# Reordered first loads, paired K and V loads, a hinted end branch and a rearranged last block in a grouped-query attention kernel

## The chip, the cores and the metric

The kernel runs on one core of a Trainium2 chip. The metric is device time in microseconds (us) of one execution; the median over several executions is compared. Besides that there is one profiled execution, whose trace gives the rows used here.

## What is computed

Two independent problems, A and B, have the same shapes. Each takes x (16 batches, 80 rows, 576 columns), a K and a V cache (16 batches, 16 heads, 512 positions, 128 deep), and the matrices Wq (576 x 4096) and Wo (4096 x 576), all in bf16. There are 32 query heads, two to each K/V head.

```python
q = (x @ wq).reshape(B, Sq, Hq, Dh).transpose(0, 2, 1, 3)
k = jnp.repeat(k_cache, rep, axis=1)
v = jnp.repeat(v_cache, rep, axis=1)
scores = jnp.einsum("bhqd,bhkd->bhqk", q, k) * (Dh ** -0.5)
p = softmax(scores, axis=-1)
o = jnp.einsum("bhqk,bhkd->bhqd", p, v)
result = o.transpose(0, 2, 1, 3).reshape(B, Sq, Hq * Dh) @ wo
```

The two results stand side by side in the output (16, 80, 1152).

## The kernel before

The work is cut into 128 **units** U: one batch and four K/V heads. U runs over the two problems, then four groups of heads (`q`), then 16 batches. Each unit loads one K block (`ldk`, a DMA transpose of 512 KB into one of five slots of `kT`) and one V block (`ldv`, a plain DMA of 512 KB into one of three slots of `v_in`), which POOL copies into one of five slots of `v_sb` (`vp`). Four units make a window W (32 of them), and eight units make an output block h8 (16 of them).

On TensorE (PE) these jobs alternate:

- `qp m.i`: one of 8 Q projections of block m (four batches), five matmuls over 576 rows of x and Wq, evacuated into `qT`. Chunks 0 to 3 of x come from one DMA transpose (`ldx`), the fifth from another (`ldx..b`).
- `s n`: three score matmuls, followed by an exponential on ScalarE (ACT) into `P`.
- `pv U.g`: four matmuls of P and V over the first 128 query columns; `pr W`: the remaining 32 columns of four units in 64 small matmuls. VectorE (DVE) then takes the reciprocal of the row sums and scales (`rcp`, `nrm`).
- `tr W.u`: four PE transposes, copied by DVE into `oM` or, for u = 4, into `oR`.
- `op h8.n`: eight matmuls with Wo. n counts five tiles `ti` with two halves `ch` each. Tile 4 reads `oR`, the others `oM`. DVE or ACT adds the result into `acc`; in the last head group the sum goes to `osb`, from which stores (`st`) write the output.

All the order is fixed when the program is built. Every operation has a **key**, a virtual time in which a unit takes 16; the operations of each engine are issued in the order of keys, and a class `_Sched` derives the semaphore waits from what is read and written. An engine never passes a waiting instruction of its own. The constants that set keys are lists at the top: `X_T` for x blocks, `K_T` and `V_T` for the first K and V loads, `WO_T` and `W1_T` for Wo of the first head group and Wq of the second, `Q_T` (start, step) for Q blocks 1 to 7, `OP_T` for output block 0. Loads beyond these lists follow a formula in U. Evacuations and stores are placed after their PE job (`place_followers`). The PE jobs other than scores and PV rotate through three PSUM banks (`JB`).

Two DMA queues are used for loads: SP's, with all K and x loads, most weights and the first 20 V blocks (`NVS`), and ACT's, with the other V blocks, Wo of the first group and Wq of the second (`W1_T`). In the first Wq load (three column pieces, `WQ0`, each in two DMAs) the first piece is on ACT's queue and two on SP's. Stores go on SP; at the very end also on ACT and POOL. A tile-4 store is eight DMAs of 16 rows.

PE begins with `NWARM` warm-up matmuls. At the end, a check of all reciprocals gives a flag; each engine loads it and branches: normally past a complete second kernel (`_general`) that stands in the code for the case that the check fails.

Of the kernel before, what the change touches and what calls it, by code (L numbers as in the profile page):

```python
# [13 lines left out]
LA = 14  # L14
# [8 lines left out]
NWARM = 10  # L23
# [594 lines left out]
def bass_concat_heads__gqa_block_cached__gqa_block_cached__near_ridge_kernel(  # L618
# [27 lines left out]
    K_T = (-798.0, -793.5, -791.7, -793.4, -793.0)  # L646
    NVS = 20
    V_T = (-798.3, -794.5, -787.0, -6.0, 10.0, 26.0, 42.0, 50.0)
    WO_T = (-12.0, -1.0, 23.0, 42.0)
    Q_T = ((-79.0, 2.0), (-59.0, 1.5), (1.0, 3.9), (163.3, 6.5), (237.3, 7.5), (299.3, 8.0), (360.3, 8.0))  # L650
    OP_T = (76.0, 10.5)
    W1_T = (-20.8, 63.0, 77.0, 99.9, 118.0)
    WQ0 = ((0, 256), (256, 512), (512, 1024))
    JB = (5, 6, 7)

# [25 lines left out]
    sem_names = (["e_pe", "e_act", "e_dve", "e_pool", "d_outp", ]  # L681
# [37 lines left out]
    jobs = []  # L719
    stores = {}  # L720
# [25 lines left out]

    add("pool", -900, em_ones, writes=[R(("ones",), 0)], name="ones")
# [7 lines left out]
    for xb in range(8):  # L755
        prob, c = divmod(xb, 4)
        x_ap = probs[prob][0].rearrange("b s d -> (b s) d")[c * QN:(c + 1) * QN, :]
        sl = xb % NX

        def em_ldx(e, x_ap=x_ap, sl=sl):  # L760
            return e.dma_start_transpose(xT[:, sl, 0:4, :], x_ap[:, 0:512].rearrange("n (c d) -> n c d", d=128))  # L761

        def em_ldx2(e, x_ap=x_ap, sl=sl):
            return e.dma_start_transpose(xT[:, sl, 4, :], x_ap[:, D - 128:D])  # L764

        t = X_T[c] if prob == 0 else 16.0 * (36, 46.5, 50, 54)[c] + 9.0
        add("sp", t, em_ldx, writes=[R(("xT", sl, 0), xb)], dsem="d_x%d" % sl, name="ldx%d" % xb)
        add("sp", t + (0.1 if xb else -0.1), em_ldx2, writes=[R(("xT", sl, 1), xb)], dsem="d_x%d" % sl,
            name="ldx%db" % xb)

    for goct in range(2 * NOCT):
        prob, q = divmod(goct, NOCT)
        wq_ap, wo_ap = probs[prob][3][:, q * 1024:(q + 1) * 1024], probs[prob][4][q * 1024:(q + 1) * 1024, :]
        sl = goct % 2
        if goct == 0:
            for hf, (n0, n1) in enumerate(WQ0):
                def em_a(e, wq_ap=wq_ap, n0=n0, n1=n1):
                    return e.dma_start(wq_sb[:, 0, 0:4, n0:n1], wq_ap[0:512, n0:n1].rearrange("(c p) n -> p c n", p=128))

                def em_b(e, wq_ap=wq_ap, n0=n0, n1=n1):  # L780
                    return e.dma_start(wq_sb[64:128, 0, 4, n0:n1], wq_ap[512:576, n0:n1])

                add("act" if hf == 0 else "sp", -799.6 + 0.2 * hf, em_a, writes=[R(("wq", 0, hf, "a"), 0)], dsem="d_wi%d" % hf, name="ldwa0.%d" % hf)
                add("act" if hf == 0 else "sp", -799.5 + 0.2 * hf, em_b, writes=[R(("wq", 0, hf, "b"), 0)], dsem="d_wi%d" % hf, name="ldwb0.%d" % hf)
        else:
            for ck in range(5):
                def em_w(e, wq_ap=wq_ap, sl=sl, ck=ck):
                    if ck < 4:
                        return e.dma_start(wq_sb[:, sl, ck, :], wq_ap[128 * ck:128 * ck + 128, :])
                    return e.dma_start(wq_sb[64:128, sl, 4, :], wq_ap[512:576, :])  # L790

                wr = [R(("wq", sl, ck), goct)]
                if goct == 2:
                    wr += [R(("wq", 0, hf, ab), 1) for hf in range(3) for ab in "ab"] if ck == 0 else []
                add("sp" if goct > 1 else "act", 256.0 * (goct - 1) + 16.0 + 20.0 * ck if goct > 1 else W1_T[ck], em_w,
                    writes=wr, dsem="d_wq%d" % sl, name="ldw%d.%d" % (goct, ck))
        for pc in range(4):
            def em_wo(e, wo_ap=wo_ap, sl=sl, pc=pc):
                return e.dma_start(wo_sb[:, sl, 2 * pc:2 * pc + 2, :],
                                   wo_ap[256 * pc:256 * pc + 256, :].rearrange("(h p) n -> p h n", p=128))  # L800

            t = 256.0 * goct - 56.0 + 22.0 * pc
            add("sp" if goct else "act", t if goct else WO_T[pc], em_wo, writes=[R(("wo", sl, pc), goct)], dsem="d_wo%d" % sl,
                name="ldwo%d.%d" % (goct, pc))

    for m in range(2 * NOCT * 4):
# [4 lines left out]
        for i in range(8):  # L811
# [22 lines left out]
            else:  # L834
                rd = [R(("wq", wsl, ck), goct) for ck in range(5)]
            job(t, em_qp, rd + [R(("wqz",), 0)] + [R(("xT", xsl, k_), xb) for k_ in range(2)],
# [38 lines left out]
    for U in range(NSU):  # L875
# [15 lines left out]

        t_k = T0 - 16.0 * (NK - 1) - LA + 1.5 if U >= NK else K_T[U]
        t_p = T0 - 12.0 if U % 4 == 1 else T0 - 18.0
        t_v = (T0 - 16.0 * NV - 8.0) if U >= NVS else (T0 - 54.0) if U >= 8 else V_T[U]
# [101 lines left out]
    for h8 in range(NH8):  # L996
# [3 lines left out]
        for n in range(10):  # L1000
            ti, ch = divmod(n, 2)
            if h8 == NH8 - 1 and ti > 2:
                ti = 7 - ti
            r = 5 * hb + ti
            t = (128.0 * h8 + 66.0 + 12.8 * n if h8 else OP_T[0] + OP_T[1] * n)
            slot = (5 * hb + n // 2) % NOSB
# [32 lines left out]
            last = h8 == NH8 - 1 and n >= 8  # L1039
            if q == NOCT - 1 and (ch == 1 or last):  # L1040
                pcs = [(64 * k_, 64, 8 * hb + 2 * ti + k_, 0) for k_ in range(2)] if ti < 4 else \
                    [(16 * k_, 16, 8 * hb + k_, 64) for k_ in range(8)]
                for pi, (p0, pn, b, s0) in enumerate(pcs):
                    c0, c1 = (ch * DC, (ch + 1) * DC) if last else (0, D)

                    def em_st(e, p0=p0, pn=pn, b=b, s0=s0, slot=slot, prob=prob, c0=c0, c1=c1):
                        return e.dma_start(out[b, s0:s0 + pn, prob * D + c0:prob * D + c1],
                                           osb[p0:p0 + pn, slot, c0:c1])

                    se = "sp" if h8 < NH8 - 1 or ti < 3 else (("sp", "act", "pool")[pi % 3] if ti == 4 else ("sp", "act")[pi])  # L1050
                    stores.setdefault("op%d.%d" % (h8, n), []).append(
                        (se, em_st, [R(("osb", slot, k_), (prob, r)) for k_ in ((ch,) if last else range(2))],
                         "d_outp" if se == "pool" else "d_out%d" % slot, "st%d.%d.%d" % (prob, r, pi)))

    jobs.sort(key=lambda j: (j[0], j[1]))
    for k, (key, _, emit, reads, name, ver, evac) in enumerate(jobs):
        bank = JB[k % 3]
        jo = add("pe", key, lambda e, emit=emit, bank=bank: emit(e, bank), reads=reads, writes=[R(("ps", bank), ver)],
                 name=name, dur={"qp": 0.68, "op": 0.98, "tr": 0.228}[name[:2]])
        for eng, ek, em, rd, wr, _d in evac:  # L1060
# [36 lines left out]
    tc = 128.0 * (NH8 - 1) + 66.0 + 12.8 * 6 + 1.5  # L1097
# [5 lines left out]
    add("pe", 128.0 * (NH8 - 1) + 66.0 + 12.8 * 7 + 2.0, em_c3, reads=[R(("okb",), 0), R(("ones",), 0)],  # L1103
        writes=[R(("ps", 0), ("C",))], name="chk3")
    add("dve", 128.0 * (NH8 - 1) + 66.0 + 12.8 * 7 + 5.0, em_c4, reads=[R(("ps", 0), ("C",))], writes=[R(("flag",), 0)], name="chk4")
# [13 lines left out]
    g_bar = nc.alloc_semaphore("g_bar")  # L1119

# [3 lines left out]
    def run(e, name):  # L1124
        for op in ops:
            if op.eng != name:
                continue
            for ck, v in op.waits:
# [7 lines left out]
        if name == "sp":  # L1136
            for i in range(NOSB):
                e.wait_ge(sems["d_out%d" % i], S.totals[("d", "d_out%d" % i)])
            e.wait_ge(sems["d_outp"], S.totals[("d", "d_outp")])
        with e.If_eq(regs[name], 0):  # L1140
            e.drain().then_inc(g_bar, 1)
            e.wait_ge(g_bar, 5)
            g_run(e, name)

# [50 lines left out]
```

## Time and profile before

| | us |
|---|---|
| median of 14 runs | 709.79 |
| lowest and highest run | 699.66 and 724.73 |
| profiled execution | 703.75 |
| its span | 701.7 |

| engine | busy us | share of the span |
|---|---|---|
| PE matmuls | 677.7 | 97% |
| PE weight loads | 581.1 | 83% |
| DVE | 393.2 | 56% |
| ACT | 377.2 | 54% |
| POOL | 243.4 | 35% |

How to read the lines that follow: PE's busy time overlaps its weight loads (PEld). A line of a group names source line, engine and operation, the tile written and the tiles read, a count and times; in brackets stands the idle time just before and what ended it. In the answer on waits the columns are total us, number of times and longest. A table by stretches gives busy us per engine (with counts), then the clock that PE was granted as a share of full speed, the share of the 16 DMA engines in use (over 1 where packets of several queues overlap) and GB/s. "SPq" and "ACTq" are the instruction queues of SP and ACT. Landing times of single DMAs are those of their last semaphore increment in the trace, counted from the span's start.

### The profile page before, as it was taken

How to read it: one execution, taken by the hardware profiler on the slowest of the kernel's cores; microseconds unless marked ns; L12 is line 12 of the kernel's file. 1: busy time of each engine (PE TensorE's matmuls, PEld its weight loads, DVE VectorE, ACT ScalarE, POOL GpSimd, SP SyncE). 2: the span in 40 equal slices, each digit the busy share in tenths (PEclk: the TensorE clock that was granted, in tenths of full speed). 3: DMA queues.
4: the chain of work that ended last, by engine and by line, in shares of the span. 5: the costliest groups of instructions: out<-in, count | busy, mean ns of one | idle time of the engine just before them, and what ended most of it. 6: DMA issues, size and time to landing. Idle time of an engine off the chain costs nothing.

```text
span 701.7 us, 21212 instructions
## 1 busy us (share of the span) xinstructions
PE 677.7 (97%) x9355; PEld 581.1 (83%) x9355; DVE 393.2 (56%) x990; ACT 377.2 (54%) x728; POOL 243.4 (35%) x138
## 2 busy tenths in 40 slices
PE   8797999999999999999999999999999999999995
PEld 4586888888888888888888788888888888888893
DVE  2442455566666666566666444556666666566663
ACT  1265666555555555555555556665555555555560
POOL 2142343532244332234433234343234442234430
PEclk9989999999999999999999999999999999999999
DMA  9999999999999999999999999999999989999841
GB/s 208 215 259 201 234 245 266 249 252 267 243 266 223 238 226 249 285 231 246 227 246 241 197 240 234 273 229 248 232 232 254 252 193 219 245 228 213 213 109 40
DMA packets 366100, 160.79 MB, mean 229 GB/s; under 512 B 283824, under 2 KB 361968, under 8 KB 366000
## 3 DMA queue, kind: packets, MB, share of 16 engines
q1 hardware_dynamic: 306304, 99.90, 77.7%
q10 hardware_dynamic: 59632, 59.41, 27.7%
q8 instruction: 75, 1.23, 0.7%
q14 instruction: 25, 0.20, 0.1%
q0 software_dynamic: 64, 0.04, 0.0%
HBM read 85.98 MB, written 2.95 MB: 127 GB/s over the span
## 4 chain that ended last, share of the span: by engine, by line
PE 88%; DMA 5%; SPq 4%; DVE 1%; issue 0%; POOL 0%; POOLq 0%
PE ps L823 22%; PE ps L1013 21%; PE ps L850 19%; PE ps L917 16%; PE ps L976 5%; PE ps L933 5%; DMA kT<-in_A_k_cache_dram 3%; SPq L883 2%; DMA kT<-in_B_k_cache_dram 2%; SPq L761 1%; DMA v_in<-in_A_v_cache_dram 1%; SPq L764 1%; DVE o_sb L957 1%; DVE osb L1035 0%; POOL v_sb L890 0%
## 5 line engine op out<-in xcount | busy, mean ns | idle before, releaser
L855 ACT ACTIVATE P<-ps 128x480 bf16<-128x480 f32 (+1 forms) x683 | 360.2, 570 | 268.2 <-PE ps L850 263.9
L890 POOL COPY v_sb<-v_in 128x2048 bf16<-128x2048 bf16 x128 | 239.6, 1893 | 435.3 <-PE ps L933 279.4
L850 PE MATMUL ps<-qT,kT 128*128 128x160 bf16 x2048 | 244.4, 233 | 9.2 <-DMA kT<-in_A_k_cache_dram 6.3
L823 PE MATMUL ps<-xT,wq_sb 128*128 128x320 bf16 x1280 | 214.2, 301 | 1.6 <-DMA wq_sb<-in_A_wq_dram 0.9
L917 PE MATMUL ps<-v_sb,P 128*128 128x130 bf16 x2048 | 203.9, 221 | 2.8 <-POOL v_sb L890 2.4
L830 DVE CAST qT<-ps 128x320 bf16<-128x320 f32 x252 | 131.1, 520 | 125.5 <-PE ps L823 124.1
L850 PEld LDWEIGHTS ps<-qT,kT 128*128 128x128 bf16 x2048 | 160.1, 98 | 27.9 <-issue 8.1
L917 PEld LDWEIGHTS ps<-v_sb,P 128*128 128x128 bf16 x2048 | 148.2, 98 | 10.4 <-POOL v_sb L890 2.8
L823 PEld LDWEIGHTS ps<-xT,wq_sb 128*128 128x128 bf16 x1280 | 118.0, 98 | 36.1 <-ACT qT L830 1.2
L1013 PE MATMUL ps<-wo_sb,oM 128*128 128x288 bf16 x1024 | 146.9, 287 | 0.1
L957 DVE TENSOR_TENSOR o_sb<-ps,rinv 128x384 bf16<-128x384 f32 (+1 forms) x224 | 120.7, 539 | 7.7
L1013 PEld LDWEIGHTS ps<-wo_sb,oM 128*128 128x128 bf16 x1024 | 96.8, 98 | 21.8 <-DVE oM L983 0.3
L983 DVE COPY oM<-ps 128x512 bf16<-128x512 bf16 x128 | 54.1, 422 | 52.4 <-PE ps L976 52.3
L1030 DVE TENSOR_TENSOR acc<-ps,acc 128x288 f32<-128x288 f32 x80 | 36.6, 458 | 48.4 <-PE ps L1013 48.4
L952 DVE RECIPROCAL rinv<-ps 128x3 f32<-128x3 f32 (+1 forms) x224 | 38.7, 173 | 44.2 <-PE ps L933 26.7
L976 PE MATMUL ps<-ident,o_sb 128*128 128x128 bf16 x640 | 60.3, 220 | 0.3 <-DVE o_sb L957 0.2
L976 PEld LDWEIGHTS ps<-ident,o_sb 128*128 128x128 bf16 x640 | 44.4, 98 | 2.2 <-DVE o_sb L957 0.6
L933 PE MATMUL ps<-v_sb,P 128*32 128x130 bf16 x2048 | 36.5, 223 | 1.2 <-DVE o_sb L957 1.0
L1013 PE MATMUL ps<-wo_sb,oR 128*128 128x288 bf16 x256 | 36.4, 286 | 0.6 <-DVE oR L990 0.6
L933 PEld LDWEIGHTS ps<-v_sb,P 128*32 128x32 bf16 x2048 | 30.7, 97 | 5.7 <-DVE o_sb L957 2.0
L1025 ACT COPY acc<-ps 128x288 f32<-128x288 f32 x40 | 15.9, 398 | 28.5 <-PE ps L1013 27.0
L1035 DVE TENSOR_TENSOR osb<-ps,acc 128x288 bf16<-128x288 f32 x40 | 18.3, 457 | 22.1 <-PE ps L1013 22.1
(24 smaller groups left out, 53.1 us busy)
## 6 DMA issues: line engine op xcount, KB each, us to landing
v_in<-in_B_v_cache_dram ACTq DMA_DIRECT2D x64, 512.0 KB, 5.2
v_in<-in_A_v_cache_dram ACTq DMA_DIRECT2D x44, 512.0 KB, 6.1
v_in<-in_A_v_cache_dram SPq DMA_DIRECT2D x20, 512.0 KB, 4.9
wo_sb<-in_B_wo_dram SPq DMA_DIRECT2D x16, 288.0 KB, 5.4
wq_sb<-in_B_wq_dram SPq DMA_DIRECT2D x16, 256.0 KB, 5.5
wo_sb<-in_A_wo_dram SPq DMA_DIRECT2D x12, 288.0 KB, 4.8
wq_sb<-in_A_wq_dram SPq DMA_DIRECT2D x9, 256.0 KB, 5.5
out_dram<-osb SPq DMA_DIRECT2D x30, 72.0 KB, 4.4
```

Source lines behind the costliest of these rows:

```text
L823: last = e.matmul(ps[:, bank, 0:QN], lhsT=wq_sb[:, wsl, ck, i * 128:(i + 1) * 128], rhs=xT[:, xsl, ck, :], start=(ck == 0), stop=(ck == 4))
L830: return e.copy(dst, src) if ev == "act" else e.tensor_copy(dst, src)
L850: last = e.matmul(ps[:, sbk, c * 160:(c + 1) * 160], lhsT=kT[:, U % NK, j, g * 128:(g + 1) * 128], rhs=qT[:, (U // 4) % NQ, U % 4, g, :], ...
L855: return e.activation(P[:, psl, 0:k, :], ps[:, sbk, 0:k * 160].rearrange("p (c n) -> p c n", c=k), AF.Exp, scale=SCALE)
L890: return e.tensor_copy(v_sb[:, vps, :, 0:128], v_in[:, vs, :, :].rearrange("p g (j d) -> p (g j) d", j=4))
L917: last = e.matmul(ps[:, bank, off:off + OP_], lhsT=pap(16 * U + 4 * g + j, 0, 128), rhs=v_sb[:, vps, 4 * g + j, :], start=(j == 0), stop=( ...
L933: last = e.matmul(ps[32 * g:32 * g + 32, bank, off:off + OP_], lhsT=pap(16 * U + 4 * g + j, 128, 160), rhs=v_sb[:, U % NVP, 4 * g + j, :], ...
L952: return e.reciprocal(rinv[:, c0:c0 + nt], ps[:, bank, 128:128 + OP_ * (nt - 1) + 1:OP_])
L957: return e.tensor_tensor(o_sb[:, osl, 0:nt, :], src, sc, AluOpType.mult)
L976: last = e.transpose(psb[:, bank, 128 * n_:128 * n_ + 128], o_sb[:, F % NOF, pos, :], ident[:])
L983: return e.tensor_copy(oM[:, osl2, :, 128 * b8:128 * b8 + 128], psb[:, bank, 0:512].rearrange("p (g c) -> p g c", g=4))
L1013: last = e.matmul(ps[:, bank, 0:DC], lhsT=w, rhs=wo_sb[:, wsl, i, ch * DC:(ch + 1) * DC], start=(i == 0), stop=(i == 7))
```

## The change

It changes orders, one warm-up length, how the last tile is stored, and how the end branch is written. No matrix work is removed except two warm-up matmuls.

- **First loads.** `ldx0` goes ahead of `ldx0b`, which gets a semaphore of its own (`d_xi`). All three pieces of the first Wq load go on ACT's queue, after an exponential of one column (`table`) that loads ACT's table. Q jobs 0 to 2 of block 0 are split in four matmuls, and one more matmul each (`qp0.ir`) once the fifth chunk is there.
- **K and V loads.** New lists give, on SP: x0, x0b, x1, x1b, v0, k0, x2, x2b, k4, v1, x3, x3b, k1, k3, k2, v2, v3, k5, v4, v5, v6, k6, k7, v7, k8, v8, v9, k9, k10, k11, v10, v11, and pairs of K and pairs of V up to unit 19. Before it was: x0b, x0, Wq0, x1, x1b, v0, k0, x2, x2b, v1, x3, x3b, k1, k3, k4, k2, v2, v3, k5, v4, k6, v5, k7, v6, v7, k8, k9, v8, k10, v9, k11 and so on in turn.
- **Weights and Q jobs.** Two pieces of the first Wo and the last two of the second Wq come at later keys; Q blocks 3 to 6 at earlier keys, block 7 is stretched.
- **POOL copies** get other keys; they stay in the same order.
- **Last output block.** Its ten jobs get keys from `LAST_T`, in the order 0, 1, 2, 3, 4, 5, 6, 8, 9, 7, with tile 3 as jobs 6 and 7.
- **Stores.** A tile-4 store is one DMA for all eight batches, everywhere; POOL stores nothing.
- **End.** The branch is a direct compare-and-branch, and a hint for it is placed in each engine's stream at the first operation with a key over 1024, about half-way.

```diff
-NWARM = 10
+NWARM = 8
+HINT_T = 1024.0
-    K_T = (-798.0, -793.5, -791.7, -793.4, -793.0)
+    K_T = (-798.0, -793.5, -791.7, -793.4, -795.5, 3.5, 35.0, 36.2, 67.0, 87.5)
+    KVP = (-61.0, -52.0)
-    V_T = (-798.3, -794.5, -787.0, -6.0, 10.0, 26.0, 42.0, 50.0)
-    WO_T = (-12.0, -1.0, 23.0, 42.0)
-    Q_T = ((-79.0, 2.0), (-59.0, 1.5), (1.0, 3.9), (163.3, 6.5), (237.3, 7.5), (299.3, 8.0), (360.3, 8.0))
+    V_T = (-798.3, -794.5, -788.3, -6.0, 10.0, 26.0, 28.0, 36.5, 67.8, 68.0)
+    WO_T = (-12.0, 2.0, 23.0, 50.0)
+    Q_T = ((-79.0, 2.0), (-59.0, 1.5), (-2.0, 3.9), (151.3, 4.5), (197.3, 7.5), (279.3, 8.0), (368.3, 9.0))
-    W1_T = (-20.8, 63.0, 77.0, 99.9, 118.0)
+    W1_T = (-20.8, 63.0, 77.0, 125.9, 134.0)
+    LAST_T = (6.0, 19.0, 46.0, 60.0, 63.0, 73.6, 78.0, 84.0, 80.0, 82.0)
...
+    add("act", -799.45, em_table, reads=[R(("ones",), 0)], writes=[R(("ri", 0), "t")], name="table")
...
-        add("sp", t + (0.1 if xb else -0.1), em_ldx2, writes=[R(("xT", sl, 1), xb)], dsem="d_x%d" % sl,
+        add("sp", t + 0.1, em_ldx2, writes=[R(("xT", sl, 1), xb)], dsem="d_x%d" % sl if xb else "d_xi",
...
-                add("act" if hf == 0 else "sp", -799.6 + 0.2 * hf, em_a, ...)
+                add("act", -799.6 + 0.2 * hf, em_a, ...)
...
+            if m == 0 and i < 3:
+                def em_q4(e, bank, i=i):
+                    last = None
+                    for ck in range(4):
+                        last = e.matmul(ps[:, bank, 0:QN], lhsT=wq_sb[:, 0, ck, i * 128:(i + 1) * 128],
+                                        rhs=xT[:, 0, ck, :], start=(ck == 0), stop=False)
+                    return last
+                def em_q5(e, bank, i=i):
+                    return e.matmul(ps[:, bank, 0:QN], lhsT=wq_sb[:, 0, 4, i * 128:(i + 1) * 128],
+                                    rhs=xT[:, 0, 4, :], start=False, stop=True)
+                later["qp0.%d" % i] = (-92.0 + 0.1 * i, em_q5, [R(("wqz",), 0), R(("xT", 0, 1), 0)])
...
-        t_k = T0 - 16.0 * (NK - 1) - LA + 1.5 if U >= NK else K_T[U]
-        t_p = T0 - 12.0 if U % 4 == 1 else T0 - 18.0
-        t_v = (T0 - 16.0 * NV - 8.0) if U >= NVS else (T0 - 54.0) if U >= 8 else V_T[U]
+        t_k = T0 - 16.0 * (NK - 1) - LA + 1.5
+        if U < NVS:
+            t_k = K_T[U] if U < len(K_T) else 32.0 * (U // 2) + 0.5 * (U % 2) + KVP[0]
+        t_p = T0 - (40.0, 16.0, 32.0, 40.0)[U % 4]
+        t_v = (T0 - 16.0 * NV - 8.0) if U >= NVS else 32.0 * (U // 2) + 0.5 * (U % 2) + KVP[1] if U >= len(V_T) else V_T[U]
...
-            if h8 == NH8 - 1 and ti > 2:
-                ti = 7 - ti
+            if h8 == NH8 - 1:
+                t = 64.0 * (NW - 1) + LAST_T[n]
...
-                pcs = [(64 * k_, 64, 8 * hb + 2 * ti + k_, 0) for k_ in range(2)] if ti < 4 else \
-                    [(16 * k_, 16, 8 * hb + k_, 64) for k_ in range(8)]
+                for pi in range(2 if ti < 4 else 1):
+                    if ti < 4:
+                        dst = out[8 * hb + 2 * ti + pi, 0:64, prob * D + c0:prob * D + c1]
+                        src = osb[64 * pi:64 * pi + 64, slot, c0:c1]
+                    else:
+                        dst = out[8 * hb:8 * hb + 8, 64:SQ, prob * D + c0:prob * D + c1]
+                        src = osb[:, slot, c0:c1]
-                    se = "sp" if h8 < NH8 - 1 or ti < 3 else (("sp", "act", "pool")[pi % 3] if ti == 4 else ("sp", "act")[pi])
+                    se = "act" if last and (ti == 3 and pi or ti == 4 and ch == 1) else "sp"
...
+            if name not in hints and op.key > 1000.0 + HINT_T:
+                hints[name] = e.mark_branch_hint_location()
...
-        with e.If_eq(regs[name], 0):
+        e.br_ne(regs[name], 0, "fast_end_" + name, "general_" + name).branch_hint(hints[name])
+        with e.bass.body("general_" + name, valid_engines=[e.engine]):
             e.drain().then_inc(g_bar, 1)
             e.wait_ge(g_bar, 5)
             g_run(e, name)
+            e.br("fast_end_" + name)
+        e.bass.switch_bb("fast_end_" + name)
```

## The prediction

> **What bounds the kernel now.** I read the busy shares, then TensorE's waits, then stretches of time, then SP's queue. First the page's first section:
>
> ```profile
> PE 677.7 (97%) x9355; PEld 581.1 (83%) x9355; DVE 393.2 (56%) x990; ACT 377.2 (54%) x728; POOL 243.4 (35%) x138
> ```
>
> TensorE (PE) is the bound. The change removes none of its work of weight, so it can only take away PE's idle time, its half-speed time and the edges. The waits of PE:
>
> ```profile
> PE ps L850 <- DMA kT<-in_A_k_cache_dram: 6.3, 2, 4.2
> PE ps L917 <- POOL v_sb L890: 2.4, 2, 1.6
> PE ps L850 <- DMA kT<-in_B_k_cache_dram: 2.4, 2, 1.4
> PE ps L823 <- DMA wq_sb<-in_A_wq_dram: 0.9, 1, 0.9
> ```
>
> The stretches (time, busy us with counts of PE, PEld, DVE, ACT, POOL, then PE clock, DMA share, GB/s) place them:
>
> ```profile
> 0.00:6.00 6.00, 4.42 (x10) 1.31 (x10) 0.27 (x1) 1.28 (x1) 2.61 (x8) 1.00 0.64 144
> 24.00:34.00 10.00, 6.81 (x71) 5.18 (x68) 3.60 (x8) 5.16 (x10) 0.00 (x0) 1.00 1.12 237
> 34.00:41.00 7.00, 5.54 (x31) 4.10 (x32) 1.60 (x4) 1.71 (x3) 3.15 (x2) 0.51 1.09 262
> ...
> 56.00:62.00 6.00, 4.45 (x57) 3.88 (x55) 1.59 (x4) 3.49 (x9) 3.79 (x2) 1.00 0.97 98
> ...
> 64.80:68.20 3.40, 3.40 (x24) 2.84 (x24) 0.42 (x1) 1.14 (x2) 0.00 (x0) 0.50 1.18 289
> ...
> 86.00:400.00 314.00, 314.00 (x4413) 272.56 (x4411) 186.56 (x469) 176.84 (x341) 114.17 (x61) 1.00 1.14 245
> 400.00:412.00 12.00, 9.61 (x163) 8.09 (x162) 4.83 (x13) 5.79 (x12) 5.62 (x3) 1.00 1.24 195
> ```
>
> Up to about 86 us the DMA engines are full and PE waits for K and V; twice its clock falls to half. From 86 to 685 PE is full but for 2.4 us near 405. The edges come last. So four places can pay: 0 to 86, the wait near 405, the last matmuls, and what follows them.
>
> **Start, 0 to 24.** The first x block now goes ahead of its fifth chunk, all Wq0 pieces go by ACT's queue, and block 0's first three Q jobs begin with four chunks. Q starts at 6.14 now (x0's second transpose landed 6.05, its issue 1.74 long). Issued first, x0 should land near 5.0, and two warm-up matmuls less (0.43 each) end the warm-up by then. But qp0.4 waits for the last Wq0 piece, landed 10.43. The Trainium skill ("DMA: Bandwidth & Descriptors", "Issuing engines are not separate DMA queues") says that issuing from several engines saves issue time alone. On SP that is 0.58+0.58+0.58+0.52 = 2.3 us, and by it all later loads would come 2.3 us sooner. The row speaks against even that: SP's issues of K last 2.2 to 4.7 us where a small x issue takes 1.24, so SP waits for engines that are full (share 1.00 from 6 us on), not for itself. Only the 0.64 of the first 6 us leaves room. Bounds -0.5 (x1 now shares the engines with Wq0) and +0.9; I take 0.3. The ACT table load of 1.28 us now stands ahead of Wq0's second piece, which still issues near 3.4 instead of 3.89.
>
> **Loads, 24 to 44.** SP's order after x2 is now k4, v1, x3, k1, k3, k2, v2 (was v1, x3, k1, k3, k4, k2, v2). K2 is last of the same set, so it lands near 35 as before (35.33). Before, PE stood through one wait:
>
> ```profile
> 30.85 0.40 PE L917 MATMUL ps<-v_sb,P 128*128 128x130 bf16 x4
> 35.46 0.56 PE L850 MATMUL ps<-qT,kT 128*128 128x160 bf16 x3 [4.21 <-DMA kT<-in_A_k_cache_dram]
> ```
>
> After: a K or V takes 2.1 to 2.4 us of DMA, so x3 lands at 26.3 and K1 at 29.0, not 26.26. PE waits 0.3 for x3, 1.9 for K1, then has 4.7 us of work and waits 1.3 for K2 at 35.0. The same end, but no single wait of 4.2 us. After s10 PE had 7.73 us to pv2.0, of which 5.44 at half clock (2.7 lost), and one Q job (0.68) now lies ahead of K2: 4.3 us, so pv2.0 at 39.4 instead of 43.19, **3.8 us gained**. This rests on the clock. The skill ("TensorE: Matmul & The Clock Gate", "Why this matters for your kernels") wants no idle gap over about 3 us. The row is harsher: after a wait of only 2.12 us at 62.6 the clock was 0.50 from 64.8 to 68.2. By the page 3.8; by the row 1.7 less (half of 3.4). I start from the page, since 1.9 is below both, and keep 2.1 as the lower end.
>
> **44 to 86.** SP now issues v4, v5, v6, k6, k7, v7, k8, v8, v9, k9 (was v4, k6, v5, k7, v6, v7, k8, k9, v8, k10). At 245 GB/s (14.2 us for 3.47 MB, v4 to v7) a K or V takes 2.14, a Wo piece 1.2, a Wq piece 1.07. V6 is two places earlier, so pv6.0's wait of 1.6 goes. K6 lands near 51.2 instead of 48.36 and wo0.3 is issued eight key units (1.2 us) later: op0.0 and s32 wait 2.0 together, s32 at 51.2 against 53.13. K7 (54.4) and V7 are in time; s37 is 3.5 ahead. K8 then lands at 59.6 against a need at 59.2, where it landed at 64.57, because DMA moved 98 GB/s from 56 to 62, when K8 and K9 shared the engines with a Wq1 piece. That slump cost about 3.3 us at K8; whether it comes again I can't read. Without it s42 is 5.1 ahead, the half clock after it goes, K9 holds 1.4, pv9.0's 0.85 goes: 6.3 ahead at s55. There stands the **new wait**: Q jobs of block 4 come 12 keys earlier (151.3), while the last two Wq1 pieces are issued 26 and 16 keys later. ldw1.4 leaves ACT about 4.75 us ahead of qp4.0 and landings of these pieces took 5.7 (last), 6.7 and 7.8 us. PE is in order, so all scores and PV behind qp4.0 stand too: 1 to 3 us, I take 1.5. Net 4.8, with the slump back 1.6. Between them I take **4.0**; it holds one quarter of a slump. From 86 on K had 4 to 7 us of slack and V 1 to 4; the load stream comes some 5 us earlier as well, so it keeps up. The earlier Q jobs of blocks 5 and 6 shift work only. vp keys on POOL move, not their order: nothing.
>
> **Stores, near 405.** A last-tile store was eight DMAs of 16 rows, now one. On SP:
>
> ```profile
> 386.58 0.57 SPq L789 DMA_DIRECT2D wq_sb<-in_B_wq_dram  x1
> 387.19 5.39 SPq L1047 DMA_DIRECT2D out_dram<-osb  x8
> 392.63 3.32 SPq L883 DMA_TRANSPOSE kT<-in_B_k_cache_dram  x1
> 395.99 0.57 SPq L789 DMA_DIRECT2D wq_sb<-in_B_wq_dram  x1
> ```
>
> The eight hold ldk73, which landed at 402.75 when PE had waited. Its slot's last reader was done ten microseconds before. One store of about 0.6 lets it go 4.8 us sooner, and ldk74 after it. The two waits (2.4) should go; bounds 0 and 2.4, I take **2.2**.
>
> **Last matmuls.** Before, PE waited 0.76 ahead of pr31, 0.11 and 0.63 ahead of op15.6 (for the oR copy). Now op15.3 (0.98) stands ahead of pr31, op15.5 between tr31.3 and tr31.4, and op15.6 on the tile that doesn't need oR ahead of op15.8. That covers 1.5; with two op jobs taken out from among the exps, ten scores and their PVs (4.6 of PE) run against ten exps (5.2 on ACT): 0.5 back. The last stores are fewer on ACT, whose last landed 698.68 beside SP's 697.94: 0.2. Sum **1.2**, bounds 0 and 2.
>
> **The branch.** After the last landing SP's branch runs, then the jump over the general kernel. The branch's line:
>
> ```profile
> L1140 SPq COMPARE_BRANCH  x1: 58/58/58, 698.7 to 698.7; - x1
> ```
>
> and the answer for the line after it (first and last start, us):
>
> ```profile
> L1145 ACTq DRAIN  x1: 62/62/62, 700.9 to 700.9; - x1
> L1145 SPq DRAIN  x1: 66/66/66, 701.4 to 701.4; - x1
> ```
>
> 58 ns of branch, then 2.6 us until SP's next instruction; on ACT 3.4. A hint is planted at key 1024, half-way. If it holds over 300 us, the target is there: 0 or 2.6, no row between; the wait is nothing but the jump, so I take **2.5**.
>
> **Sum:** 0.3 + 4.0 + 2.2 + 1.2 + 2.5 = 10.2 us. The profiled execution, 703.75 (span 701.7 and 2.05 around it), would become 693.6. The median shown is 709.79, 6.0 above it; the same sum off the median is **699.6**, 1.4% less.
>
> **Rivals.**
> (1) *The start is bound by DMA anyway.* The slump of 56 to 62 comes again and the waits of 1.9 at K1 and K8 halve the clock as at 62.6: 4.0 becomes 1.6 - 1.7, about 0. For it: SP issues without a pause up to 110 us in the trace, and no byte is removed. Against: pv6.0 and the 4.2 wait are matters of order. Time 703.6.
> (2) *The hint doesn't hold.* Every engine runs hundreds of instructions between hint and branch. Against: the rows show nothing else in those 2.6 us that an early fetch would leave. Time 702.1.
> (3) *Slower: Wq1 comes late at qp4.0.* Price: 1 us for each us that ldw1.4 lands after 4.75, and the half clock (1.7). ldw1.2, in the slump, took 10.4 (51.9 to 62.4). No gain is left once the landing takes 4.75 + 1.5 + 10.2 - 1.7 = 14.8; at 18 the time is 713. For it: both last pieces are now issued together, among K9 to K11. Against: longer than any landing of a piece in the trace.
>
> **Numbers.** About 1% is what a measurement of this kernel can tell from no change. Forecast 0.54, (1) 0.21, (2) 0.16, (3) 0.09. Below 702.7: nearly all of the forecast, half of (2), a little of (1): 0.64. Above 716.9: the far part of (3), with a spread of runs from 699.66 to 724.73: 0.07. Within: 0.29. The bounds add up to 0.9 + 6.3 + 2.4 + 2 + 2.6 = 14.2, so 695.6 at best; medians of few runs scatter by some 4 us: 691 below, 709 above, which takes in (1) and (2).
>
> **Signs in the profile after.** K1's wait near 27 and K2's near 34, both under 2.5, clock full from 34 to 41; no eightfold store on SP near 390 and no wait for B's K; PE without a wait at pr31; SP's DRAIN within 0.3 of its branch. Wrong if qp4.0 shows a wait for Wq of over 4 us, if DMA stays near 100 GB/s through K8, or if over 2 us still lie between branch and DRAIN.

## The result, and the profile after

The changed kernel takes **695.51 us** (median of 10 runs, 690.15 to 717.38); beside it the kernel before takes 706.30 (47 runs). The ratio is **0.9875**, 95% interval 0.9836 to 0.9914, so 8.8 us of 706 with an interval of 6.1 to 11.6. Ratios leave out runs that lie well above the fastest of their kernel (the profiled run of a_k14 below is one of those), medians hold all. Predicted was 699.6 off 709.79, a ratio of 0.986. The profiled execution took 690.99 (span 689.2, before 701.7).

The first section of the page after. PE's work is the same within the two warm-up matmuls; its share of the span is 98% where it was 97%, because the span is shorter:

```profile
PE 673.5 (98%) x9353; PEld 578.3 (84%) x9353; DVE 393.2 (57%) x990; ACT 377.5 (55%) x729; POOL 241.9 (35%) x136
```

PE's waits after (total us, times, longest). The waits on V (POOL) and on B's K are gone; K of problem A has five short waits where it had two of up to 4.2; there are new waits for Wo and x:

```profile
PE ps L874 <- DMA kT<-in_A_k_cache_dram: 4.3, 5, 1.3
...
PE ps L1039 <- DMA wo_sb<-in_A_wo_dram: 1.6, 1, 1.6
...
PE ps L848 <- DMA xT<-in_A_x_dram: 1.3, 1, 1.3
...
PE ps L831 <- DMA wq_sb<-in_A_wq_dram: 0.6, 2, 0.4
```

The same stretches as before the change (time, busy us with counts of PE, PEld, DVE, ACT, POOL, PE clock, DMA share, GB/s). Read the clock column first: 0.51 at 34 to 41 and 0.50 at 64.8 to 68.2 have become 1.00. Then GB/s at 56 to 62: 252 for 98. Then PE's busy time at 400 to 412: full:

```profile
0.00:6.00 6.00, 3.57 (x8) 1.02 (x8) 0.27 (x1) 1.49 (x2) 2.62 (x8) 1.00 0.76 160
...
34.00:41.00 7.00, 6.41 (x84) 5.82 (x85) 3.46 (x9) 4.53 (x9) 3.73 (x2) 1.00 1.12 316
...
56.00:62.00 6.00, 6.00 (x80) 5.52 (x78) 2.01 (x6) 4.25 (x11) 3.08 (x2) 1.00 1.22 252
...
64.80:68.20 3.40, 3.31 (x44) 2.90 (x42) 1.21 (x3) 1.88 (x5) 0.98 (x1) 1.00 1.19 122
400.00:412.00 12.00, 12.00 (x142) 10.46 (x140) 5.42 (x14) 7.85 (x16) 3.03 (x2) 1.00 1.04 245
```

SP's queue near the last stores of problem A: one store of 0.66 us stands where the eightfold one of 5.39 us was, and K transposes follow each other:

```profile
378.47 0.66 SPq L1078 DMA_DIRECT2D out_dram<-osb  x1
...
383.37 0.58 SPq L797 DMA_DIRECT2D wq_sb<-in_B_wq_dram  x1
384.00 3.75 SPq L907 DMA_TRANSPOSE kT<-in_B_k_cache_dram  x1
387.79 0.59 SPq L798 DMA_DIRECT2D wq_sb<-in_B_wq_dram  x1
388.43 14.94 SPq L907 DMA_TRANSPOSE kT<-in_B_k_cache_dram  x4
```

And the end: SP's branch, then its next instruction, 0.54 us later where 2.69 lay between:

```profile
L1176 SPq COMPARE_BRANCH  x1: 78/78/78, 688.4 to 688.4; - x1
...
L1184 SPq DRAIN  x1: 53/53/53, 689.0 to 689.0; - x1
```

PE near its end. Before, it waited ahead of pr31 (the 64 small matmuls) and ahead of the output matmuls that read `oR`:

```profile
686.99 1.14 PE L933 MATMUL ps<-v_sb,P 128*32 128x130 bf16 x64 [0.76 <-DVE o_sb L957]
...
690.58 2.13 PE L1013 MATMUL ps<-wo_sb,oR 128*128 128x288 bf16 x16 [0.63 <-DVE oR L990]
```

After, pr31 has no wait, and from 670 us on there is one left, at a transpose:

```profile
673.37 0.40 PE L1002 MATMUL ps<-ident,o_sb 128*128 128x128 bf16 x4 [0.46 <-DVE o_sb L983]
...
677.41 1.13 PE L959 MATMUL ps<-v_sb,P 128*32 128x130 bf16 x64
```

**Stages.** For what follows, the start of single score jobs on PE was read off the trace by counting matmuls in program order. The table has every kernel that ran. s0 is the first score job, s55 is the one behind which the new Q order puts block 4's first job, s100 lies behind the last start-up wait. "100-200" is the time from s100 to s200, and so on; "tail" goes from s600 to the end of the last matmul, "end" from there to the end of the span. The last column is the ratio to the kernel before, run beside it, with its interval.

| kernel | s0 | s10 | s55 | s100 | 100-200 | 200-352 | 352-400 | tail | end | ratio |
|---|---|---|---|---|---|---|---|---|---|---|
| before | 24.41 | 35.46 | 78.49 | 120.34 | 96.98 | 148.44 | 49.03 | 85.22 | 7.0 | |
| b_again | 24.59 | 35.83 | 76.09 | 118.07 | 97.06 | 148.91 | 47.40 | 85.21 | 7.0 | 1.0026 [0.9960, 1.0092] |
| b_hint | 24.90 | 35.80 | 78.62 | 121.67 | 96.97 | 148.44 | 47.22 | 85.21 | 5.9 | 0.9968 [0.9871, 1.0065] |
| b_store | 23.85 | 35.46 | 77.45 | 119.45 | 104.77 | 148.85 | 46.42 | 85.22 | 7.5 | 1.0036 [0.9952, 1.0121] |
| b_kv | 24.76 | 36.22 | 77.27 | 119.11 | 96.97 | 153.61 | 46.92 | 85.21 | 7.3 | 1.0015 [0.9946, 1.0084] |
| b_kvwq | 24.83 | 36.10 | 72.33 | 115.86 | 99.34 | 148.51 | 53.31 | 85.23 | 7.3 | 1.0001 [0.9954, 1.0048] |
| after | 25.10 | 34.59 | 71.49 | 115.07 | 96.19 | 148.46 | 46.43 | 84.16 | 4.2 | 0.9875 [0.9836, 0.9914] |
| a_first | 24.89 | 36.29 | 71.03 | 114.60 | 101.64 | 148.44 | 46.42 | 84.16 | 4.5 | 0.9918 [0.9877, 0.9959] |
| a_oldord | 25.49 | 34.49 | 75.57 | 117.41 | 97.14 | 148.47 | 46.42 | 84.14 | 4.6 | 0.9894 [0.9814, 0.9975] |
| a_k14 | 26.68 | 35.04 | 73.65 | 116.87 | 101.65 | 152.33 | 46.42 | 84.14 | 4.5 | 0.9881 [0.9842, 0.9920] |
| a_warm | 26.37 | 35.92 | 72.17 | 115.53 | 95.61 | 148.47 | 46.43 | 84.15 | 4.4 | 0.9904 [0.9868, 0.9941] |
| a_w14 | 26.61 | 36.28 | 75.16 | 118.47 | 98.43 | 148.44 | 46.42 | 84.16 | 4.3 | 0.9829 [0.9761, 0.9897] |
| a_nk6 | 25.51 | 36.67 | 72.21 | 115.64 | 103.84 | 148.72 | 46.42 | 84.14 | 4.6 | 0.9871 [0.9783, 0.9959] |
| a_hint0 | 27.16 | 35.22 | 72.32 | 115.74 | 96.24 | 148.45 | 46.42 | 84.15 | 4.4 | profile only |

Kernels that begin with b_ are the kernel before with one part added, those with a_ the changed kernel with one part taken back or altered. From s400 to s600 every one of the fourteen takes 194.67 to 194.69 us: PE alone sets that time. All differences between these profiles come from the start, from two regions of K waits (100 to 200 and 200 to 352), from 352 to 400, and from the end.

One column needs care. The new `Q_T` puts two more Q jobs ahead of s100 (245 Q matmuls stand ahead of it instead of 235). They take 1.4 us: without waits, 100-200 is 96.97 with the old Q jobs and 95.61 with the new ones. So a kernel with the new Q jobs (b_kvwq, and all a_ kernels but a_oldord and a_w14) has done 1.4 us more work at s100, and 1.4 us is added to its gain there below. At s55 the work is equal.

### The profile page after: what moved, and what is told of

It reads as the page before. It is cut to its first block, busy times and chain, and to the rows that moved or that the text cites. A ratio compares the mean times of both kernels' runs of the same rounds, so it can differ in the third digit from the quotient of the medians.

```text
span 689.2 us, 21189 instructions
## 1 busy us (share of the span) xinstructions
PE 673.5 (98%) x9353; PEld 578.3 (84%) x9353; DVE 393.2 (57%) x990; ACT 377.5 (55%) x729; POOL 241.9 (35%) x136
## 4 chain that ended last, share of the span: by engine, by line
PE 89%; DMA 5%; SPq 4%; DVE 1%; issue 0%; ACT 0%
PE ps L831 22%; PE ps L1039 22%; PE ps L874 19%; PE ps L943 16%; PE ps L1002 5%; PE ps L959 5%; DMA kT<-in_A_k_cache_dram 4%; SPq L907 2%; DMA wq_sb<-in_A_wq_dram 1%; SPq L769 1%; SPq L772 1%; DVE o_sb L983 0%; DVE osb L1061 0%; SPq L911 0%; DVE xT L1112 0%
## 5 line engine op out<-in xcount | busy, mean ns | idle before, releaser
L831 PE MATMUL ps<-xT,wq_sb 128*128 128x320 bf16 x1265 | 209.8, 299 | 0.9 <-DMA wq_sb<-in_A_wq_dram 0.6
L831 PEld LDWEIGHTS ps<-xT,wq_sb 128*128 128x128 bf16 x1265 | 115.9, 97 | 33.2 <-issue 0.7
L1051 ACT COPY acc<-ps 128x288 f32<-128x288 f32 x40 | 15.9, 398 | 28.3 <-PE ps L1039 28.3
```

What stands on the lines that cost most here:

```text
L831: last = e.matmul(ps[:, bank, 0:QN], lhsT=wq_sb[:, wsl, ck, i * 128:(i + 1) * 128], rhs=xT[:, xsl, ck, :], start=(ck == 0), stop=(ck == 4))
```

## The experiments

Where an expectation says "unit 55", "unit 32" or "unit 2", the job s55, s32 or pv2.0 is meant.

### The kernel before again (b_again)

No edit. It tells which of the features read as typical belong to the order and which to one execution.

> The kernel before, unchanged, for a second trace. Theory A (the slump of the DMA engines to about 100 GB/s from 56 to 62 us came by chance): this trace shows no such slump, K8 lands near 61 instead of 64.6, and pv9.0 (PE's last wait of the start, 76.8) comes up to 3 us sooner. Theory B (the slump belongs to this order of loads, K8 and K9 sharing the engines with a piece of Wq1): it is there again, under 150 GB/s, within 2 us of the same place. Both: ratio to the kernel before 1.000 within 0.4%, and 2.6 us between SP's branch and its next instruction.

Its stretches:

```profile
34.00:41.00 7.00, 5.17 (x29) 3.81 (x30) 1.24 (x4) 1.71 (x3) 3.06 (x2) 0.56 1.15 275
...
56.00:62.00 6.00, 5.32 (x71) 4.76 (x69) 1.75 (x5) 4.37 (x10) 3.46 (x2) 1.00 1.16 138
```

The half clock at 34 to 41 and the slump at 56 to 62 come again (138 GB/s; 164 and 147 in b_hint and b_store). They belong to the kernel before and not to one execution. The order of K and V alone doesn't make them: a_oldord below has it too, with other first loads, at full clock and 212 GB/s. What doesn't come again is the size of single waits: K8 held PE for 0.58 instead of 2.12 us, the waits near 405 were 0.82 in all instead of 2.39.

### The hint alone (b_hint)

```diff
-        with e.If_eq(regs[name], 0):
+        e.br_ne(regs[name], 0, "fast_end_" + name, "general_" + name).branch_hint(hints[name])
...
```

> The kernel before with the hinted end branch alone. Theory (the jump's 2.6 us are the fetch of code that the hint brings ahead): from SP's branch to its next instruction 0.5 us or less instead of 2.6, ratio 0.997. Rival (the other edits of the end brought the gain; the hint is forgotten on the way): 2.6 us stay, ratio 1.000.

```profile
L1144 SPq COMPARE_BRANCH  x1: 78/78/78, 699.3 to 699.3; - x1
```

SP's DRAIN began at 699.82, 0.54 after the branch; without a hint five profiles have 2.65 to 2.94. So 2.2 us of the branch go. The time from the last matmul fell by less, from about 7.2 to 5.9, because the last store landed 5.1 us after it in this run (4.0 to 4.3 in the five without a hint). The ratio is too wide to tell 0.3% from nothing.

### One store instead of eight, alone (b_store)

```diff
-                    [(16 * k_, 16, 8 * hb + k_, 64) for k_ in range(8)]
+                    ([(16 * k_, 16, 8 * hb + k_, 64) for k_ in range(8)] if h8 == NH8 - 1 else [None])
...
```

(None makes one DMA for the eight batches.)

> The kernel before with each tile-4 store, except those of the last output block, as one DMA in place of eight. Theory (the eight stores hold SP, so ldk73 and ldk74 land late): no wait of PE for B's K near 405 (2.4 us before), PE there 2.4 us sooner relative to 390 us, ratio 0.997. Rival (the K loads around 400 are late because the DMA engines are full with Wq5): the waits stay, or move to the next K, ratio 1.000.

From s352 to s400 it took 46.42 us, as every kernel with the single store; the five kernels with eight stores took 46.92 to 53.31. So the mechanism is shown. But this profile lost more elsewhere, at another K:

```profile
125.47 0.41 PE L917 MATMUL ps<-v_sb,P 128*128 128x130 bf16 x4 [0.90 <-POOL v_sb L890]
126.79 0.38 PE L850 MATMUL ps<-qT,kT 128*128 128x160 bf16 x3 [0.47 <-ACT P L855]
142.33 0.56 PE L850 MATMUL ps<-qT,kT 128*128 128x160 bf16 x3 [4.39 <-DMA kT<-in_A_k_cache_dram]
```

That K was issued at 124.02 and landed at 142.19, 18 us later, while its stretch from 130 to 140 moved 157 GB/s (246 in the kernel before).

### K and V order alone (b_kv)

`K_T`, `KVP`, `V_T` and the formulas of `t_k`, `t_p`, `t_v` as changed; all else as before.

> The kernel before with the new order of K and V loads alone; first loads, Wo, Wq1 and the Q jobs stay. Theory (the order of loads makes the start's gain): no wait over 2.5 us for K2, clock full from 34 to 41 us, no wait at pv6.0; PE's last wait of the start ends 5 us or more ahead of 76.8; ratio 0.992 to 0.995. Rival (the gain needs the later Wq1 pieces and the earlier Q jobs): K9 or K10 land as late as before and the last wait ends at 74 or later, ratio 0.997 to 1.000.

The clock is full from 34 to 41 as foreseen, and K2 makes no wait. But a wait of 3.43 has moved to K1, and others follow:

```profile
30.07 0.56 PE L851 MATMUL ps<-qT,kT 128*128 128x160 bf16 x3 [3.43 <-DMA kT<-in_A_k_cache_dram]
...
51.50 1.16 PE L1016 MATMUL ps<-wo_sb,oM 128*128 128x288 bf16 x8 [1.49 <-DMA wo_sb<-in_A_wo_dram]
54.25 0.37 PE L851 MATMUL ps<-qT,kT 128*128 128x160 bf16 x3 [1.15 <-DMA kT<-in_A_k_cache_dram]
...
70.36 0.37 PE L851 MATMUL ps<-qT,kT 128*128 128x160 bf16 x3 [2.39 <-DMA kT<-in_A_k_cache_dram]
```

s100 starts at 119.11, within the 118.07 to 121.67 of the old order. By s100 and by the ratio the rival holds: this part alone brings next to nothing. Its sign does not hold, for the last wait of the start ended at 70.36 and not at 74 or later; the clock fell to half behind it.

### All orders, but nothing else (b_kvwq)

```diff
 (as b_kv, and)
-    WO_T = (-12.0, -1.0, 23.0, 42.0)
+    WO_T = (-12.0, 2.0, 23.0, 50.0)
-    W1_T = (-20.8, 63.0, 77.0, 99.9, 118.0)
+    W1_T = (-20.8, 63.0, 77.0, 125.9, 134.0)
 (and Q_T as changed)
```

> The kernel before with the whole order of the early loads and Q jobs as changed (K, V, Wo, Wq1, Q jobs), and nothing else: first loads, stores, last jobs and branch as before. Theory (K and V order pays only together with the Wq1, Wo and Q moves, and needs no first loads): s100 at 114.5 to 116, as in the changed kernel with the first loads of before (114.60), where the K and V order alone had 119.11; 56 to 62 us moves over 220 GB/s; ratio 0.992 to 0.995. Rival (that run's 114.60 was luck, and the order pays only with the first loads): s100 at 117.5 to 119, ratio 0.997 to 1.001.

At s100 the theory's number stands: 115.86, and 114.60 in a_first with the same start, against a mean of 119.88 in four profiles of the kernel before: 4.7 us on average of the two, **6.0 us** with the 1.4 for the two Q jobs. From 56 to 62 the core moves 236 GB/s. Still the ratio is 1.0001. The profile shows places where the gain went. From s352 to s400 it took 6.9 us more than the 46.42 of a free PE. Two of the three waits there come after a store in eight parts:

```profile
393.14 3.67 SPq L1050 DMA_DIRECT2D out_dram<-osb  x8
```

The largest one, with 3.4 us of half clock behind it, comes before that store: its K landed 11.4 us after its issue, while 380 to 387 moved 156 GB/s (228 in the kernel before).

```profile
387.01 0.37 PE L851 MATMUL ps<-qT,kT 128*128 128x160 bf16 x3 [2.38 <-DMA kT<-in_B_k_cache_dram]
...
405.04 0.37 PE L851 MATMUL ps<-qT,kT 128*128 128x160 bf16 x3 [1.30 <-DMA kT<-in_B_k_cache_dram]
...
417.02 0.37 PE L851 MATMUL ps<-qT,kT 128*128 128x160 bf16 x3 [1.11 <-DMA kT<-in_B_k_cache_dram]
```

Between s100 and s200 it lost 3.7 us more, against the 95.61 of a free PE. One profile can't say whether all the runs lose it there.

### First loads as before, all else changed (a_first)

The diff's edits to `ldx`, `ldwa0`, `ldwb0`, `table`, `NWARM` and the split Q jobs taken back.

> The changed kernel with its first loads put back as they were before (fifth chunk of x block 0 first, two of three Wq0 pieces on SP, ten warm-up matmuls, block 0's Q jobs in one piece, no early table load). Theory A (the first loads are worth most through the load stream, because SP, freed of four Wq0 pieces, comes to v0 and K0 about 3.5 us sooner): the first score starts 0.6 sooner than in the changed kernel's 25.10, but K1 lands near 29.9 instead of 28.3, K6 near 54 instead of 51.7, K8 near 62 instead of 59.2, and the score of unit 55 starts at 73 to 75 instead of 71.5; ratio to the kernel before 0.989 to 0.991. Theory B (as the prediction had it: the stream doesn't move, the edit costs the 0.7 by which the first score came late): K1, K6 and K8 land where they do in the changed kernel, unit 55 starts at 70.8, ratio 0.986 to 0.987.

In the profile theory B stands: K6 landed at 51.14, K8 at 59.46, and s55 started at 71.03. K1's 29.81 looks like theory A, but five profiles of the new order with the new first loads have 28.3 to 30.3. The ratio, 0.9918, lies where theory A had it and above theory B's; its interval meets that of the changed kernel, so whether the first loads bring anything in the runs is open. This profile lost 6.0 us between s100 and s200. Against b_kvwq, which has the same start and differs in stores, last jobs and end alone, the ratio moves from 1.0001 [0.9954, 1.0048] to 0.9918 [0.9877, 0.9959]: these three parts are worth about 0.8%, 5.9 us, with an interval of some 1.5 to 10.

### Orders as before, all else changed (a_oldord)

> The changed kernel with all orders of K, V, Wo, Wq1 and Q jobs put back as before; first loads, stores, last jobs and hint stay changed. Theory A (first loads feed the stream, and order and first loads add up): K2's wait is near 2.7 instead of 4.2, unit 55 starts at 75 to 76 (before order: 76.1 to 78.6 in four profiles; changed: 71.5), 56 to 62 us moves under 170 GB/s as in every profile of that order; ratio 0.991 to 0.993. Theory B (only the order counts at the start): unit 55 starts at 77.5 to 78.5, ratio 0.993 to 0.996. If the order gave nothing, as the run of the K and V order alone could be read: unit 55 near 72, ratio 0.987.

s55 at 75.57 and K2's wait of 2.17 fit theory A. The slump was milder than expected (212 GB/s), but the waits on V came back, with half clock behind the long one:

```profile
34.49 0.37 PE L873 MATMUL ps<-qT,kT 128*128 128x160 bf16 x3 [2.17 <-DMA kT<-in_A_k_cache_dram]
...
57.09 0.41 PE L940 MATMUL ps<-v_sb,P 128*128 128x130 bf16 x4 [3.54 <-POOL v_sb L913]
```

```profile
34.00:41.00 7.00, 6.51 (x80) 5.72 (x81) 3.72 (x9) 4.07 (x8) 3.73 (x2) 1.00 1.10 237
56.00:62.00 6.00, 4.91 (x41) 4.37 (x42) 1.07 (x3) 2.57 (x5) 2.92 (x2) 0.72 0.98 212
```

So in this one profile the first loads alone take 2.5 us off s100 (117.41 against a mean of 119.88 in four); on top of the new order they take nothing that shows (115.07, 115.74 and 115.64 against 115.86 and 114.60).

### K4 and V1 back at their old places (a_k14)

```diff
-    K_T = (-798.0, -793.5, -791.7, -793.4, -795.5, 3.5, ...
+    K_T = (-798.0, -793.5, -791.7, -793.4, -793.0, 3.5, ...
-    V_T = (-798.3, -794.5, -788.3, ...
+    V_T = (-798.3, -794.5, -787.0, ...
```

> The changed kernel with K4 and V1 back at their old places (order v1, x3, K1, K3, K4, K2). Theory (the clock falls with one long wait and not with two short ones): one wait for K2 of 3 us or more, clock under 0.85 from 34 to 41, PV of unit 2 starts at 41 or later instead of 39.0, of which K6's wait at 51.8 takes some back: ratio 0.988 to 0.991. Rival (the load stream sets the time and K2 lands at the same moment): clock full, PV of unit 2 within 0.5 of 39.0, no difference at unit 32 (51.8), ratio 0.987.

At K2 the theory fails: one wait, but of 1.11, clock 1.00 from 34 to 41, pv2.0 at 39.48 (39.03 in the changed kernel). The rival's "no difference at unit 32" fails as well: K6 landed at 53.51 (51.65), and PE waited 3.54 for it, with half clock behind. K2 landed at 34.90; in all fourteen profiles it landed between 34.35 and 36.14, whatever stood before it. How long PE waits for it depends on when PE comes, and here PE came late (s0 at 26.68).

### Eleven warm-up matmuls (a_warm)

```diff
-NWARM = 8
+NWARM = 11
```

> The changed kernel with eleven warm-up matmuls instead of eight, so that TensorE isn't idle between their end (4.92) and the first Q job (6.20). Theory (the gap of 1.28 put the clock's rise from 6.8 to 9.4 us): clock full by 7 us, first score at 24.3 to 24.6 instead of 25.10, ratio 0.986 to 0.987 where the changed kernel has 0.9875. Rival (Q waits for Wq0's last piece, landed 11.38, whatever the clock): first score within 0.25 of 25.10.

Worse than both: s0 at 26.37. x0 landed at 5.24 and Q ran at full clock, but only to the next wait, for the last Wq0 piece, and after that at half clock:

```profile
11.12 13.11 PE L831 MATMUL ps<-xT,wq_sb 128*128 128x320 bf16 x83 [1.79 <-DMA wq_sb<-in_A_wq_dram]
```

```profile
11.00:12.00 1.00, 0.88 (x6) 0.61 (x7) 0.00 (x0) 0.00 (x0) 0.00 (x0) 0.81 1.10 311
12.00:15.00 3.00, 3.00 (x13) 1.74 (x12) 0.65 (x2) 0.52 (x1) 1.89 (x1) 0.50 1.08 248
```

The same happens with eight warm-up matmuls. In three of those six profiles x0 landed by 5.63; PE then waited 1.75 to 2.35 for the last piece, ran at half clock behind it, and s0 came at 26.6 to 27.2. In the other three x0 landed at 5.99 or later; the last piece cost 0.17 to 0.72, the clock stayed full, and s0 came at 25.1 to 25.5. So an earlier x0 gains nothing here as long as the last Wq0 piece comes no sooner (10.98 to 11.80 in all seven). The changed kernel's own profile is one of the second three (x0 at 6.07, a wait of 0.38).

### Wo, Wq1 and Q jobs as before (a_w14)

`WO_T`, `W1_T` and `Q_T` taken back in the changed kernel.

> The changed kernel with the orders of Wo, Wq1 and the Q jobs as before; K and V order, first loads, stores, last jobs and hint stay changed. Score s100 starts at 115.1 in the changed kernel, 117.4 with all load orders as before, 119.1 in the kernel before with the K and V order alone. Theory (K and V order pays only together with the later Wq1 pieces, which otherwise share the engines with K8 to K10): waits for K8 or K10 of over 1 us in sum, s100 at 116.5 to 118, ratio 0.989 to 0.992. Rival (the K and V order with the first loads does all of it): s100 at 115 to 115.5, ratio 0.987.

s100 at 118.47 is late as the theory had it (4.4 us behind the 115.48 of the changed kernel's start, with the two Q jobs counted), but not by the waits it named: PE waits for K6, and later for V. The Wo and Wq1 order pays, but that it does so by keeping K8 to K10 free is not shown:

```profile
54.81 0.37 PE L874 MATMUL ps<-qT,kT 128*128 128x160 bf16 x3 [3.16 <-DMA kT<-in_A_k_cache_dram]
...
79.10 0.41 PE L943 MATMUL ps<-v_sb,P 128*128 128x130 bf16 x4 [1.28 <-POOL v_sb L914]
```

The ratio of five runs, 0.9829, is the best of all beside a slower trace: a few runs don't rank these kernels.

### A sixth K buffer (a_nk6)

```diff
-NK = 5
-NX = 5
-NOF = 8
+NK = 6
+NX = 4
+NOF = 7
...
```

(The three dots stand for K loads of units 14 to 19 that go out earlier and x loads of B that go out later.)

> The changed kernel with six K buffers instead of five (room from four x buffers for five and seven o_sb buffers for eight); K loads from unit 20 on go out 16 keys, about 2.5 us, earlier, those of units 14 to 19 by 5 to 15 keys, and the loads of B's x blocks follow the last reading of A's. Theory (single slow K landings, as the 3.3 us waits at 129, 142, 246 and 336 us in four profiles, make runs of one kernel differ by 10 us; a longer lead covers them): no wait for K over 1 us after 130 us, the lowest time still about 690, the median 692 to 694, ratio 0.982 to 0.985, fewer runs over 700. Rival (the DMA engines themselves fall behind for a while, so an earlier issue lands no sooner): waits of 3 us for K stay, ratio 0.987 as the changed kernel.

```profile
142.40 0.37 PE L874 MATMUL ps<-qT,kT 128*128 128x160 bf16 x3 [0.57 <-DMA kT<-in_A_k_cache_dram]
149.93 0.56 PE L874 MATMUL ps<-qT,kT 128*128 128x160 bf16 x3 [2.68 <-DMA kT<-in_A_k_cache_dram]
164.19 0.37 PE L874 MATMUL ps<-qT,kT 128*128 128x160 bf16 x3 [1.83 <-DMA kT<-in_A_k_cache_dram]
```

The rival holds. 2.5 us more lead don't cover the late waits; the DMA engines as a whole moved less, with 180 GB/s from 130 to 140 and 191 from 150 to 160 (250 and 235 in the changed kernel). Why they do so in one execution and not in another stays open.

### The hint at the very start (a_hint0)

```diff
-HINT_T = 1024.0
+HINT_T = -880.0
```

> The changed kernel with the branch hint planted at the very start instead of half-way. If a hint holds over any distance: SP's DRAIN 0.5 after its branch, as with the hint half-way (0.54). If it is lost on the way: 2.7 to 2.9, as without a hint (2.65 to 2.94 in four profiles).

The hint ran on SP at 0.80 us; the branch came at 689.24 and the DRAIN at 689.78, 0.54 later. It holds over the whole kernel.

## Why the prediction was right, step by step

The sum, 10.2 us or 1.4%, lies inside the interval of 6.1 to 11.6, and the likeliest case is the one that came. The parts on stores, tail and branch came as told. The part on the start is right in sign, but four of its terms are off, in both directions; that the total came so near owes something to luck.

- **Start 0 to 24: the step failed.** It took +0.3 with bounds of -0.5 and 0.9. The first score job comes 1.5 us *later* (mean 26.09 in six profiles with the new first loads and eight warm-up matmuls, 24.60 in seven with the old ones). x0 was put near 5.0; in seven profiles it landed at 5.2 to 6.5, mean 5.75 (6.08 in the seven with the old first loads). The last Wq0 piece, put at 10.43, landed at 11.0 to 11.8 (9.8 to 10.7 with the old first loads), and PE waits for that piece, in four of the seven with half clock behind it. Why both land later than thought is argued, not shown: Wq0's second piece, now issued by ACT at 1.98 and not by SP at 3.89, shares the engines with x0, and x1 goes out 2.8 us sooner (3.50 for 6.33) beside the last piece. The table load, from 1.90 to 3.18, delayed no DMA: that second piece was put at 3.4.
- **The rule weighed there.** The Trainium skill ("DMA: Bandwidth & Descriptors", "Issuing engines are not separate DMA queues") grants a second issuing engine its issue time alone, 2.3 us here. SP did come to K0 3.8 us sooner (6.86 for 10.70). But K0 landed just 0.9 sooner (means of seven profiles each, 15.45 and 16.33) and K2 0.2 (35.17 and 35.33, over both orders). So most of the issue time doesn't reach the loads; the row was right against the rule's sum.
- **Loads 24 to 44: size right, reason half right.** pv2.0 started at 39.03 (predicted 39.4). K1's wait was 0.80 and K2's 1.29 (predicted 1.9 and 1.3), and the clock stayed full. But the new place of K4 isn't needed for it: a_k14 has the old one and nearly the same pv2.0. In all fourteen profiles it is the waits of 3.4 to 4.4 for K2 that go with half clock from 34 to 41; a later arrival of PE avoids them as well as a better order. Neither of the two readings of the clock that the step weighed is a rule (last section).
- **44 to 86: taken too small.** Predicted were 4.0, with 4.3 for the whole start. Three profiles with all of the start's changes have s100 at 115.07 to 115.74, mean 115.48, against 119.88; with the two Q jobs that is **5.8 us** for the whole start, its first stretch of -1.5 included. At s55 they are 5.7 ahead, where the step had 6.3. Two deductions did not come. The slump doesn't come again: from 56 to 62 the nine profiles with the new K and V order moved 203 to 273 GB/s, the four of the kernel before 98 to 164. And the wait at qp4.0 was 0.20, not 1.5: Wq1's last piece landed 6.1 us after its issue. The step counted K6 (0.89 waited) and Wo's last piece (1.59) together at 2.0, which measured 2.5.
- **From 86 on: the lead did not hold.** The step put this at nothing: K with 4 to 7 us of slack, and a load stream that comes as much sooner as PE. In the trace before, K of units 22 to 26 already landed only 1.5 to 3.9 us ahead of the first score job that reads it (its lead). In the changed kernel the blocks of units 25 to 28 land 3.6 us sooner than before (means of 155.9 and 152.3), but PE comes to them 7.0 us sooner, so their lead falls from 3.4 to 5.4 us to 0.1 to 1.3. In all seven profiles with the new Q, Wo and Wq1 order the smallest lead there is 0.2 or less; in six of the seven without it, 3.4 or more (1.2 in b_store, after its late K). With so little lead a late block stops PE at once; from unit 30 on the lead is over 6 us again in the changed kernel. Between s100 and s200 the seven lost 3.6 us on average and the others 1.4, but both groups scatter from 0 to 8, so that the new order loses more there is not shown.
- **What the step didn't see** is that its parts don't add up: K and V order alone gave 0.8, with Wo, Wq1 and Q moved 6.0, first loads alone 2.5 (one profile), all together 5.8. And of the 6 us at s100 the runs of b_kvwq show nothing at the end; its interval leaves at most 3.2. How much of the start's gain survives in a typical run is open. That it is lost where the lead is gone is likely, and not shown.
- **Stores, near 405: right, on thin ground.** 2.2 was read from one execution. Above the free 46.42, five profiles with eight stores lose 2.6, 1.0, 0.8, 0.5 and 6.9 (of the last, a good half before the store near 390), a mean of 2.4; nine with one store lose nothing.
- **Last matmuls: right.** The tail went from 85.2 to 84.15 in every profile with the new order of jobs: 1.07 for the 1.0 of the matmuls in the predicted 1.2.
- **The branch: right.** 2.5 was taken for branch and jump; 2.2 went there. The last store landed 3.5 us after the last matmul (mean of eight) instead of 4.1 (five), 0.6 where 0.2 was taken. So the end fell from 7.2 to 4.4: 2.8 for the 2.7 of branch and last landing together.

The rivals: the slump's return (1) is refuted by the row of 56 to 62, the lost hint (2) by the branch's rows, the late Wq1 (3) by the 0.20 at qp4.0. Stores, tail and end add up to 2.4 + 1.07 + 2.8 = 6.3 us in the traces, and to 5.9 in the ratios of a_first and b_kvwq. With the total of 8.8 this leaves 2.5 to 2.9 for the start, less than the 5.8 at s100, with intervals too wide to call the rest lost.

No version tried is shown to beat the changed kernel.

## What to carry to other kernels

Read a wait that a DMA ends from several executions before pricing it: here the same stretch lost 0.5 to 6.9 us. When PE gains at the start of a kernel that streams loads, work out by how much the loads behind gain too: here PE came 7.0 us sooner and K 3.6, and the lead was gone. Before you compare two kernels at a mark, count the work ahead of it. Here the jump over a large block of code cost 2.7 us, and a hint half-way or at the very start took 2.2 of it away.

## What the runs showed of the hardware

- **Half clock after waits.** PE's granted clock fell to 0.50, for 3.4 us or twice that, around the end of waits as short as 1.75 (a_w14, at 11.4), 1.79 (a_warm, at 11.1) and 2.12 (before, at 64.7). It stayed full after 1.88 (a_warm, at 35.9) and 2.17 (a_oldord, at 34.5), and even after 2.75 (b_hint, at 58.6), 2.85 and 3.72 (a_k14, at 163.2 and 246.1). The Trainium skill ("TensorE: Matmul & The Clock Gate", "Why this matters for your kernels") asks for no gap over about 3 us; these runs show half clock after shorter gaps and none after a longer one. The length of the last gap alone doesn't decide.
- **Branch and code.** 2.65 to 2.94 us for a taken branch over a long block (five profiles), 0.53 to 0.55 with a hint (nine), agree with the skill's statement ("Runtime: NRT & Kernel Launch", "Instruction fetch mechanics") that a jump out of the fetched pages waits for a fetch; the fetch itself no trace here shows. A hint given 688 us ahead (a_hint0) held as well as one given 336 us ahead.
- **DMA has slow spells.** A K block took 5 to 9 us from issue to landing in 92 of 128 cases of the changed kernel, and 18 us once in b_store. Between 110 and 170 some stretches of 10 us fell to 157 to 191 GB/s in b_store, a_first and a_nk6 (235 or more in the changed kernel), and these three lost 6 to 8 us on PE between s100 and s200. But a_oldord had a stretch of 192 and lost 0.2, with 3.4 us of lead or more at units 25 to 28. The cause of the spells is open.
